# The first layer of the first expert, with the loop over input chunks outside three column groups

## The chip, the cores and the metric

The kernel runs on one core of a Trainium2 chip. The metric is the device time of one execution in microseconds (us). Three timed runs of the kernel before took 868.44, 870.32 and 873.09 us; their median is 870.32. Times inside the kernel come from one profiled execution.

## The reference

Capped attention followed by a mixture of experts, one expert for each token, all in float32:

```python
scores = scale * q @ k.T                   # 8 batches, 12 heads, 448 positions, head size 64
scores = cap * tanh(scores / cap)
attn = softmax(scores) @ v
x = attn as (3584, 768)                    # tokens x model width
logits = x @ w_gate + modality_bias[modality_id]
e = argmax(logits); gate = softmax(logits)[e]
out = gate * (relu(x @ w1[e]) @ w2[e])     # 8 experts, 768 -> 1024 -> 768
```

## The kernel before, in words

**Stages.** Attention comes first, in 24 units (`ND`) of two head pairs each, seven steps (`STEPS`) a unit, 168 steps in all. A step (`scores`, L443) has TensorE form scores, ScalarE take tanh and exp of them; `weigh` (L471) multiplies the weights with the values a few steps later, into a two-bank tile xT; `add` (L463, VectorE) sums the weights, `keep` (L486) copies xT out of PSUM, `sums` (L490) forms row sums and logits for the gate, `turn` (L501) transposes these, `logits` (L511) divides, `tokens` (L524) transposes the unit's output to token rows and writes them to the DRAM array xd. After three units a batch is complete, and `route` (L212) finds each token's expert and its place in a map in DRAM (mapd), with four indirect puts of 112 tokens each on GpSimd's queue.

Then come slots of up to 384 tokens of one expert. A slot's rows are fetched by three indirect gathers of 128 rows (`gather`, L710) through a piece of the map (mt) into xg. They are transposed in six chunks (`KC`) of 128 columns and split into a high and a low part (`transpose`, L743: ScalarE copies the high part, VectorE subtracts it from the whole to get the low). Weights are loaded by SyncE into four buffers (raw; two more, spare, for the first expert) and split likewise (`split_w`, L727). The first layer (`ffn1`, L762) has eight column groups (`FC`) of 128; each sums over six chunks three products, high by high, high by low and low by high. The second layer (`ffn2`, L793) runs six groups of 24 products.

**The seam.** The first slot belongs to an expert that has enough tokens already before the last batch. `SOON` is the unit (20 of 0 to 23) after which it is chosen. In unit 22 the map is made complete for it, `early_slot` (L292) picks it, SyncE starts to load its six first-layer chunks (`load_w1`, L558), and at step 4 of that unit GpSimd gathers its rows. Chunks 0 to 2 of its weights are split on GpSimd, chunk 3 on VectorE in unit 23, chunks 4 and 5 on ScalarE and VectorE behind the last step. After the last step, the code (L630 to L644) transposes chunks 0 to 3 into two double banks, then runs the last two `weigh`, then transposes chunks 4 and 5, adds and keeps. The first layer of the first slot then takes up what is left of attention in between: `last_sums`, `last_logits` and `last_rank` after column groups 0, 1 and 2, and the table of all later slots (`slots`, L310) after group 4. The first four second-layer weight chunks are split ahead of the column groups in program order, ScalarE casting and GpSimd subtracting (`load_w2`, L738).

**Order.** `pin` keeps an instruction in program order among the pinned ones of its engine; what isn't pinned is placed by a scheduler when the program is built. Semaphores and waits follow from which tiles are read and written. Each engine then works through its own queue in order. The first layer's products are not pinned; attention's are.

Of the kernel before, what the change touches and what calls it, by code (L numbers as in the profile page):

```python
# [69 lines left out]
W2_EARLY = 4  # L70
CAP_FAST = 64.0
# [7 lines left out]
class Program:  # L79
# [132 lines left out]
    def route(self, b, lg, pool, ps, tok=None, bank=None):  # L212

        nc = self.nc
        L = pool.tile([CP, C, E], F32, name="L")
# [26 lines left out]
        nc.vector.tensor_tensor(self.acc, before[:, C - 1], oh[:, C - 1], op=ALU.add)  # L242
        yield
# [8 lines left out]
        nc.vector.tensor_tensor(  # L252
            rows, rk.rearrange("p (c e) -> p c e", c=C), self.region[:CP].unsqueeze(1).to_broadcast([CP, C, E]), op=ALU.add
        )
        nc.vector.tensor_tensor(rows, rows, oh, op=ALU.mult)
        posf = pool.tile([CP, C], F32, name="posf")
        nc.vector.tensor_reduce(posf, rows, axis=AX.X, op=ALU.add)
        pos = pool.tile([CP, C], I32, name="pos")
        nc.vector.tensor_copy(pos, posf)

        pay = pool.tile([CP, C, 2], F32, name="pay" if tok is not None else f"pay{b % 2}")
        if tok is None:
            nc.gpsimd.iota(pay.bitcast(I32)[:, :, 0], pattern=[[1, C]], base=b * S, channel_multiplier=C)
        else:
            nc.vector.tensor_copy(pay.bitcast(I32)[:, :, 0], tok)
        gs = pool.tile([CP, C], F32, name="gs")
        nc.vector.tensor_reduce(gs, ex, axis=AX.X, op=ALU.add)
        nc.vector.tensor_scalar(gs, gs, 1e-9, None, op0=ALU.add)
        nc.vector.reciprocal(pay[:, :, 1], gs)
# [14 lines left out]
    def counts(self, pool, ps):  # L284
# [4 lines left out]
        nc.vector.tensor_copy(cnt, cps[:, :E])  # L289
# [128 lines left out]
    def attention(self, firsts, rp, xp):  # L418
        tc, nc = self.tc, self.nc
        pe, pin, V = nc.tensor, self.pin, nc.vector  # L420
        with ExitStack() as st:
            ld = st.enter_context(tc.tile_pool(name="ld", bufs=3))
            pp = st.enter_context(tc.tile_pool(name="pp", bufs=5))
            ps_s = st.enter_context(tc.tile_pool(name="ps_s", bufs=2, space=PSUM))
            ps_x = st.enter_context(tc.tile_pool(name="ps_x", bufs=1, space=PSUM))
            ps_g = st.enter_context(tc.tile_pool(name="ps_g", bufs=1, space=PSUM))

# [58 lines left out]
            def keep(d):  # L486
                kept[d] = xp.tile([128, 2, S], F32, name="xT", bufs=3)
                pin(V.tensor_copy(kept[d], self.xT[:, :, :S]))
# [60 lines left out]
            def start_route(b):  # L549
                way = self.route(b, lgs[b], rp, self.ps_r, bank=lambda: self.glog)  # L550
                next(way)
                routing[:] = [way]
# [21 lines left out]
            for n in range(END):  # L574
# [14 lines left out]
                if s == 4 and d >= 2:  # L589
                    if d - 2 == SOON:  # L590
                        self.gather(maps, known=NT - S)
                    else:
                        turn(d - 2)
# [36 lines left out]
            for n in due[END][:2]:  # L630
                weigh(n)
# [450 lines left out]
```

## Time and profile before

| | |
|---|---|
| profiled execution, its own time | 869.54 us |
| span, first to last instruction | 867.9 us |
| timed runs | median 870.32 us (868.44 to 873.09) |
| TensorE (PE) busy | 835.6 us, 96% |
| ScalarE (ACT) busy | 529.3 us, 61% |
| VectorE (DVE) busy | 515.4 us, 59% |
| GpSimd (POOL) busy | 153.2 us, 18% |
| mean granted TensorE clock | 0.990 |
| moved by DMA | 136.92 MB, 158 GB/s over the span |

A busy time says how long an engine had an instruction in work; matmuls overlap, two records at a time, so the start distance and not the duration is what one costs. The granted clock is 1.00 at 2.4 GHz and 0.50 at 1.2 GHz. A timeline row has start, duration, engine, line, operation, output <- inputs, shapes, how many instructions were merged into it and, in brackets, how long the engine had been idle before and what released it. PEld is TensorE's weight load, SP is SyncE, and a q behind an engine's name is its queue of issued instructions.

### The profile page before, as it was taken

Reading aid. Unit: us, or ns where it says so; the run is one execution under the profiler, and the core shown is the slowest. Engines: PE = TensorE matmul, PEld = TensorE weight load, DVE = VectorE, ACT = ScalarE, POOL = GpSimd, SP = SyncE. Lnnn points to the kernel's source line nnn. Section 1 sums busy time; section 2 is a strip of 40 time slices with the busy share of each in tenths; the row PEclk is TensorE's granted clock in tenths of the full one; section 3 lists DMA queues with packets and bytes.
Section 4 is the critical chain, followed back from the end, with each engine's and each line's share of the span. In section 5 each row is a group of like instructions: output and inputs, shape, how many; then the busy total and the mean of one; then the engine's idle time right before and its main releaser. Section 6 shows DMA issues by size and latency. Waiting matters only on the chain. (4 is left out here: it accounts for less than half of the span.)

```text
span 867.9 us, 15885 instructions
## 1 busy us (share of the span) xinstructions
PE 835.6 (96%) x6216; PEld 635.6 (73%) x6216; DVE 515.4 (59%) x889; ACT 529.3 (61%) x624; POOL 153.2 (18%) x161
## 2 busy tenths in 40 slices
PE   7999999999999995999999999999999999999996
PEld 2344444434444433989999999999999999989996
DVE  3679687888888788855443444234444433457851
ACT  6999999999999982244442444334344333446551
POOL 2002020202021154552020020201102030110000
PEclk9999999999999997999999999999999999999998
DMA  5353544554453664377255473534646354447650
GB/s 169 104 171 92 165 124 157 145 170 100 161 125 132 171 146 170 105 234 263 101 159 210 140 250 111 169 132 162 239 140 212 100 167 165 159 144 238 220 184 6
DMA packets 44284, 136.92 MB, mean 158 GB/s; under 512 B 8526, under 2 KB 9102, under 8 KB 44192
## 3 DMA queue, kind: packets, MB, share of 16 engines
q1 hardware_dynamic: 35008, 103.10, 37.4%
q0 software_dynamic: 9040, 32.64, 12.0%
q8 instruction: 52, 0.85, 0.4%
q14 instruction: 40, 0.33, 0.1%
q10 hardware_dynamic: 144, 0.00, 0.0%
HBM read 114.20 MB, written 22.69 MB: 158 GB/s over the span
## 5 line engine op out<-in xcount | busy, mean ns | idle before, releaser
L455 ACT ACTIVATE pt<-sc,isc 128x896 f32<-128x896 f32 x168 | 161.2, 994 | 14.4 <-PE sc L451 8.6
L781 PE MATMUL ph<-x,al 128*128 128x384 f32 (+2 forms) x528 | 166.8, 316 | 0.0
L806 PE MATMUL py<-bh,hh 128*128 128x384 f32 x464 | 158.7, 343 | 1.4 <-ACT hh L787 1.4
L806 PE MATMUL py<-bh,hl 128*128 128x384 f32 x464 | 156.3, 337 | 0.0
L806 PE MATMUL py<-bl,hh 128*128 128x384 f32 x464 | 156.0, 337 | 0.0
L458 ACT ACTIVATE pt<-pt,cabs 128x1792 f32<-128x1792 f32 x84 | 150.4, 1790 | 2.7
L481 PE MATMUL xT<-pt,va 64*64 64x448 f32 x1344 | 147.2, 542 | 0.0
L469 DVE TENSOR_TENSOR tot<-tot,pt 128x896 f32<-128x896 f32 x120 | 134.8, 1123 | 7.2 <-ACT pt L458 3.9
L777 PE MATMUL ph<-x,ah 128*128 128x384 f32 x384 | 128.9, 336 | 0.0
L778 PE MATMUL ph<-x,ah 128*128 128x384 f32 x384 | 128.6, 335 | 0.0
L481 PEld LDWEIGHTS xT<-pt,va 64*64 64x64 f32 x1344 | 50.6, 134 | 78.2 <-issue 69.0
L732 DVE TENSOR_TENSOR bl<-raw,bh 128x768 fp32r<-128x768 f32 x84 | 77.6, 956 | 48.6 <-ACT bh L731 48.4
L731 ACT CAST bh<-raw 128x768 fp32r<-128x768 f32 x88 | 70.0, 839 | 58.3 <-DMA raw<-in_w_dram 49.5
L781 PEld LDWEIGHTS ph<-x,al 128*128 128x128 f32 x528 | 100.7, 191 | 0.0
L816 POOL DMA_INDIRECT out_dram<-ot,mt x29 | 32.5, 1120 | 383.9 <-ACT ot L811 308.4
L811 ACT ACTIVATE ot<-py,mt 128x384 f32<-128x384 f32 x58 | 33.7, 581 | 98.7 <-PE py L806 53.1
L787 ACT ACTIVATE hh<-ph 128x384 fp32r<-128x384 f32 x64 | 30.5, 488 | 99.4 <-PE ph L781 95.7
L806 PEld LDWEIGHTS py<-bh,hh 128*128 128x128 f32 x464 | 87.2, 188 | 1.8 <-ACT hh L787 1.7
L732 DVE TENSOR_TENSOR al<-raw,ah 128x1024 fp32r<-128x1024 f32 x61 | 74.7, 1256 | 22.1 <-ACT ah L731 22.0
L806 PEld LDWEIGHTS py<-bl,hh 128*128 128x128 f32 x464 | 87.2, 188 | 0.3 <-DVE bl L732 0.2
L760 DVE TENSOR_TENSOR x<-ptr,x 128x384 fp32r<-128x384 f32 (+2 forms) x66 | 32.8, 517 | 92.0 <-ACT x L759 92.0
L806 PEld LDWEIGHTS py<-bh,hl 128*128 128x128 f32 x464 | 87.2, 188 | 0.2 <-DVE hl L788 0.2
(156 smaller groups left out, 1056.0 us busy)
## 6 DMA issues: line engine op xcount, KB each, us to landing
raw<-in_w_dram SPq DMA_DIRECT2D x88, 384.0 KB, 4.9
raw<-in_w_dram SPq DMA_DIRECT2D x64, 512.0 KB, 4.5
kq<-in_kq_dram SPq DMA_DIRECT2D x24, 448.0 KB, 5.6
va<-in_v_dram SPq DMA_DIRECT2D x24, 448.0 KB, 6.7
kx<-in_kq_dram SPq DMA_DIRECT2D x24, 448.0 KB, 5.8
xd<-xs POOLq DMA_DIRECT2D x23, 448.0 KB, 4.8
spare<-in_w_dram SPq DMA_DIRECT2D x2, 512.0 KB, 7.3
mapd<-pay,pos POOLq DMA_INDIRECT x32, 8.3
```

Source lines behind the costliest of these rows:

```text
L455: pin(nc.scalar.activation(weights(n), sc[:, :, :S], AF.Tanh, scale=self.isc))
L458: pin(nc.scalar.activation(pt, pt, AF.Exp, scale=self.cabs))
L469: pin(V.tensor_tensor(tots[d], pt_of(n - 1) if s == 1 else tots[d], pt_of(n), op=ALU.add))
L481: pin(pe.matmul(self.xT[j * D : (j + 1) * D, i, :S], vas[d][rows, o : o + D], pt[rows, j], start=s == 0, stop=s == STEPS - 1,))
L731: keep((cast.tensor_copy if cast else self.nc.scalar.copy)(hi, raw))
L732: keep((minus or self.nc.vector).tensor_tensor(lo, raw, hi, op=ALU.subtract))
L760: keep(nc.vector.tensor_tensor(lo, pt[:, :w], hi, op=ALU.subtract))
L777: nc.tensor.matmul(ph[:, :w], hi[:, fs], self.x[:, k, 0, :w], start=first, stop=False)
L778: nc.tensor.matmul(ph[:, :w], hi[:, fs], self.x[:, k, 1, :w], start=False, stop=False)
L781: nc.tensor.matmul(ph[:, :w], lo[:, fs], self.x[:, k, 0, :w], start=False, stop=last)
L806: nc.tensor.matmul(py[:, :HALF], self.h[a][:, f, rows], self.w2s[f][c][:, cs], start=i == 0, stop=i == 3 * FC - 1,)
L811: nc.scalar.mul(ot[:, cs], py[:, :HALF], mt[:, t, 1:2])
```

## The change

In the first slot alone, the first layer's loop over chunks now stands outside its first three column groups: for each chunk, nine products into three banks, then what has to happen before the next chunk. The other five groups run as before, one after the other. The products of the first four groups are pinned.

- `transpose` is divided into `move` (TensorE) and `take` (ScalarE and VectorE). Before the layer only chunk 0 is moved and taken, and chunks 1 and 2 moved, each into a bank of its own; chunks 3 to 5 are moved at the layer's start (`move_last`) and taken between the chunks' products (`ready`). The pool of score banks is closed earlier for that.
- Weight chunks 0 and 1 are split on VectorE alone in units 22 and 23, chunks 2 to 5 on ScalarE and VectorE, chunk 2 behind the last step and 3 to 5 between the chunks' products. GpSimd splits none of the first layer's.
- The last `keep` moves from VectorE to ScalarE, and the last four additions are divided around chunk 0.
- The gather of the first slot is issued at step 2 of unit 22, not step 4. The sums of unit 21 move from step 5 of unit 22 to step 0 of unit 23.
- What is left of attention hangs on other places: sums after chunk 2, logits after chunk 3, the last batch's routing after the three groups, its rank after group 3; the slot table stays after group 4. The second-layer weight chunks are split two after the three groups and two after group 3. Of the second layer's weight loads three are issued before the layer and one after chunk 3's split.
- In `route`, the gate weights are computed before the rank, and for the batch of the first slot the whole tail is pinned (`firm`).

```diff
@@ route
-    def route(self, b, lg, pool, ps, tok=None, bank=None):
+    def route(self, b, lg, pool, ps, tok=None, bank=None, firm=False):
+        firmly = self.pin if firm else (lambda inst: inst)
...
+        firmly(nc.vector.tensor_reduce(gs, ex, axis=AX.X, op=ALU.add))
+        firmly(nc.vector.tensor_scalar(gs, gs, 1e-9, None, op0=ALU.add))
+        firmly(nc.vector.reciprocal(pay[:, :, 1], gs))
         yield
...
+        firmly(nc.vector.tensor_reduce(posf, rows, axis=AX.X, op=ALU.add))
+        firmly(nc.vector.tensor_copy(pos, posf))
@@ attention, steps
-                if s == 4 and d >= 2:
-                    if d - 2 == SOON:
-                        self.gather(maps, known=NT - S)
-                    else:
...
+                if (d, s) == (SOON + 3, 0):
+                    sums(d - 2)
...
                     load_w1((2, 3, 4, 5))
-                    split(0, nc.gpsimd, nc.gpsimd)
-                if (d, s) == (SOON + 2, 4):
-                    split(1, nc.gpsimd, nc.gpsimd)
-                    split(2, nc.gpsimd, nc.gpsimd)
-                if (d, s) == (SOON + 3, 4):
-                    split(3, V, V)
+                    self.gather(maps, known=NT - S)
+                if (d, s) == (SOON + 2, 6):
+                    split(0, V, V)
+                if (d, s) == (SOON + 3, 5):
+                    split(1, V, V)
@@ attention, behind the last step
+            sst.close()
+            ps_m = st.enter_context(tc.tile_pool(name="ps_m", bufs=4, space=PSUM))
+            free = [ps_m.tile([128, 512], F32, name="ptr") for _ in range(4)]
+            spots = (
+                ps_g.tile([128, 512], F32, name="ptr", tag="glog"), free[3],
+                self.ps_r.tile([128, 512], F32, name="ptr", tag="small"),
+            )
+            left = due[END]
+            for n in left[:2]:
                 weigh(n)
+            for n in range(END - BEHIND, END - 2):
+                add(n)
+            self.move(0, spots[0])
+            self.take(0, spots[0], pin=True)
+            for k in (1, 2):
+                self.move(k, spots[k])
+            for n in left[2:]:
                 weigh(n)
+            keep(ND - 1, nc.scalar.copy)
+            add(END - 2)
+            add(END - 1)
+            self.take(1, spots[1], pin=True)
+            split(2, None, V)
+            self.take(2, spots[2], pin=True)
+            self.raws = [self.load_raw(self.first_e, self.w2, k, DM) for k in range(3)]
+            def move_last():
+                for k, pool in zip(range(3, KC), (self.ps_t, self.ps_t, self.ps_y)):
+                    last.append(pool.tile([128, 512], F32, name="ptr" if k < 5 else "py"))
+                    self.move(k, last[-1])
+            def ready(k):
+                if k >= 3:
+                    split(k, None, V)
+                    self.take(k, last[k - 3], pin=True)
+                if k == 3:
+                    self.raws.append(self.load_raw(self.first_e, self.w2, k, DM))
             def last_sums():
+                ready(3)
                 sums(ND - 1, self.ps_y, "py")
                 turn(ND - 2)
                 logits(ND - 2)
-                tokens(ND - 2, nc.gpsimd, *[(self.ps_t, "ptr")] * 2)
             def last_logits():
+                ready(4)
                 turn(ND - 1)
                 logits(ND - 1)
+            def last_route():
+                tokens(ND - 2, nc.gpsimd, *[(self.ps_t, "ptr")] * 2)
                 self.way = self.route(B - 1, lgs[B - 1], rp, self.ps_r)
...
+                "start": move_last, ("k", 2): last_sums, ("k", 3): last_logits, ("k", 4): lambda: ready(5),
+                ("k", KC - 1): last_route, ("f", 3): last_rank,
@@ ffn1
+        if lead:
+            hooks["start"]()
+            phs = [bank() for _ in range(lead)]
+            for k in range(KC):
+                for f in range(lead):
+                    products(phs[f], f, k)
+                if k < KC - 1:
+                    hook("k", k)
+            for f in range(lead):
+                finish(phs[f], f)
+            hook("k", KC - 1)
+        for f in range(lead, FC):
+            ph = bank()
+            for k in range(KC):
+                products(ph, f, k)
+            finish(ph, f)
+            hook("f", f)
@@ run_slot
+            early = lambda ks: self.load_w2(cur[0], raws, ks, self.nc.gpsimd)
+            for at, ks in ((("k", KC - 1), range(2)), (("f", 3), range(2, W2_EARLY))):
+                hooks[at] = lambda work=hooks[at], ks=ks: (work(), early(ks))
```

## Rows read from the trace of the kernel before

**Rows 1.** Busy time by stretches of 20 us: stretch, length, busy us (and instructions) of PE, PEld, DVE, ACT and POOL, then the mean granted TensorE clock, the share of the DMA engines and GB/s.

```profile
320.00:340.00 20.00, 10.59 (x92) 5.24 (x96) 15.31 (x15) 9.44 (x11) 12.59 (x8) 0.80 0.75 266
```

**Rows 2.** TensorE's timeline over the seam: L506 turn, L495 sums, L481 attention products, L750 transposes of token rows, L777 the first layer's first product.

```profile
319.91 0.65 PE L506 MATMUL lt<-ident,gl 128*112 128x128 f32 x4
...
322.28 0.57 PE L495 MATMUL glog<-tot,pick 128*32 128x448 f32 x2
...
323.97 3.94 PE L481 MATMUL xT<-pt,va 64*64 64x448 f32 x40
330.17 0.25 PE L750 MATMUL ptr<-identr,xg 128*128 128x128 f32 x1 [2.26 <-DMA xg<-xd,mt]
...
333.15 0.37 PE L750 MATMUL ptr<-identr,xg 128*128 128x128 f32 x1 [1.37 <-DMA xg<-xd,mt]
336.96 1.00 PE L750 MATMUL ptr<-identr,xg 128*128 128x128 f32 x6 [3.44 <-DVE x L760]
339.21 0.62 PE L750 MATMUL ptr<-identr,xg 128*128 128x128 f32 x3 [1.25 <-DVE x L760]
339.76 2.90 PE L481 MATMUL xT<-pt,va 64*64 64x448 f32 x16
...
343.13 0.41 PE L777 MATMUL ph<-x,ah 128*128 128x384 f32 x1
```

**Rows 3.** The list of waits between 326 and 344 us: who waited for whom, us in total, times, the longest.

```profile
PEld ptr L750 <- DVE x L760: 5.1, 2, 3.6
PE ptr L750 <- DMA xg<-xd,mt: 4.7, 3, 2.3
```

**Rows 4.** VectorE's timeline: L259 the places of the tokens in the map, L469 additions of attention, L731 a weight cast, L760 the low part of a transposed chunk.

```profile
303.55 0.17 DVE L259 CAST pos<-posf 112x4 int32<-112x4 f32 x1
...
308.95 1.08 DVE L469 TENSOR_TENSOR tot<-pt 128x896 f32<-128x896 f32 x1
...
310.66 7.26 DVE L469 TENSOR_TENSOR tot<-tot,pt 128x896 f32<-128x896 f32 x4
...
325.00 1.96 DVE L731 CAST ah<-raw 128x1024 fp32r<-128x1024 f32 x1 [1.97 <-DMA raw<-in_w_dram]
...
332.57 2.73 DVE L469 TENSOR_TENSOR tot<-tot,pt 128x896 f32<-128x896 f32 x1
...
336.37 0.54 DVE L760 TENSOR_TENSOR x<-ptr,x 128x384 fp32r<-128x384 f32 x1
```

**Rows 5.** ScalarE's timeline: L759 the high part of chunk 0.

```profile
333.56 0.48 ACT L759 CAST x<-ptr 128x384 fp32r<-128x384 f32 x1 [5.52 <-PE ptr L750]
```

**Rows 6.** GpSimd's timeline: L272 the puts into the map (first and fourth of one batch, fourth of the last batch), L732 a weight subtraction, L713 gathers (first and third of the first slot, first of the second), L704 the map read for the second slot.

```profile
304.53 0.99 POOL L272 DMA_INDIRECT mapd<-pay,pos  x1 [8.07 <-DVE esc L304]
...
308.36 2.49 POOL L272 DMA_INDIRECT mapd<-pay,pos  x1 [0.30 <-issue]
...
313.85 3.13 POOL L732 TENSOR_TENSOR al<-raw,ah 128x1024 fp32r<-128x1024 f32 x1
321.63 1.08 POOL L713 DMA_INDIRECT xg<-xd,mt  x1 [4.66 <-DMA mt<-mapd]
...
324.34 1.01 POOL L713 DMA_INDIRECT xg<-xd,mt  x1 [0.30 <-issue]
...
365.88 0.94 POOL L272 DMA_INDIRECT mapd<-pay,pos  x1 [0.30 <-issue]
...
371.35 0.54 POOL L704 DMA_DIRECT2D mt<-mapd  x1 [0.81 <-issue]
...
375.04 1.43 POOL L713 DMA_INDIRECT xg<-xd,mt  x1 [0.40 <-issue]
```

**Rows 7.** Busy time in short stretches, columns as in rows 1; the last three are granted clock, DMA share and GB/s.

```profile
332.00:333.00 1.00, 0.00 (x0) 0.00 (x0) 1.00 (x3) 0.00 (x0) 1.00 (x1) 0.50 0.07 28
...
340.00:342.00 2.00, 2.00 (x12) 0.56 (x12) 1.23 (x2) 1.30 (x2) 0.00 (x0) 0.50 0.00 0
342.00:344.00 2.00, 2.00 (x19) 1.41 (x12) 0.96 (x2) 0.86 (x2) 0.00 (x0) 0.96 0.00 0
```

**Rows 8.** Groups of instructions over the whole run, shapes kept apart: line, engine, operation, tiles and shapes, count, then busy us, mean ns of one, and the idle time before them.

```profile
L455 ACT ACTIVATE pt<-sc,isc 128x896 f32<-128x896 f32 x168 | 161.2, 994 | 14.4 <-PE sc L451 8.6 <-DVE meta L371 5.7
...
L732 DVE TENSOR_TENSOR al<-raw,ah 128x1024 fp32r<-128x1024 f32 x61 | 74.7, 1256 | 22.1 <-ACT ah L731 22.0
...
L731 ACT CAST ah<-raw 128x1024 fp32r<-128x1024 f32 x60 | 60.6, 1049 | 25.5 <-DMA raw<-in_w_dram 22.3 <-PE py L806 1.3 <-DVE al L732 1.3
...
L760 DVE TENSOR_TENSOR x<-ptr,x 128x384 fp32r<-128x384 f32 x54 | 29.1, 554 | 83.8 <-ACT x L759 83.8
...
L499 DVE COPY gl<-glog 128x448 f32<-128x448 f32 x24 | 14.9, 620 | 0.1
...
L732 POOL TENSOR_TENSOR bl<-raw,bh 128x768 fp32r<-128x768 f32 x4 | 7.2, 1835 | 15.0 <-ACT bh L731 15.0
```

**Rows 9.** The same table as rows 1 for the first layer of the first slot.

```profile
343.10:372.25 29.15, 29.15 (x182) 27.88 (x181) 22.71 (x92) 7.33 (x14) 13.64 (x12) 1.00 0.29 86
```

**Rows 10.** TensorE's timeline at the second slot's first transposes.

```profile
385.84 0.28 PE L750 MATMUL ptr<-identr,xg 128*128 128x128 f32 x1 [0.65 <-DMA xg<-xd,mt]
387.53 0.53 PE L750 MATMUL ptr<-identr,xg 128*128 128x128 f32 x4 [1.41 <-DMA xg<-xd,mt]
```

More of the change, by code (lines that the diff above doesn't have):

```diff
@@ L633, in attention @@
-            pair = [ps_s.tile([128, 2, 512], F32, name="ptr", tag="sc") for _ in range(2)]
-            for k in range(4):
-                move(k, pair[k // 2][:, k % 2])
-            for n in due[END][2:]:
-                weigh(n)
-            split(5, None, V)
-            move(4, self.ps_r.tile([128, 512], F32, name="ptr", tag="small"))
-            move(5, ps_g.tile([128, 512], F32, name="ptr", tag="glog"))
-            for n in range(END - BEHIND, END):
-                add(n)
-            keep(ND - 1)
@@ L741, in load_w2, with move @@
             self.split_w(raw, self.w2s[k], pin=bool(raws), minus=minus)
[L743 to L748 removed]
+    def move(self, k, pt, n=TW):
         for t in range(n):
[L750 removed]
+            move = self.nc.tensor.transpose(
                 pt.bitcast(F32R)[:, t * 128 : (t + 1) * 128], self.xg[:, t, k * 128 : (k + 1) * 128], self.identr
@@ L754, in transpose, with take, ffn1 @@
                 self.pin(move)
+    def take(self, k, pt, n=TW, pin=False):
+        nc, w = self.nc, n * 128
+        keep = self.pin if pin else (lambda inst: inst)
         hi, lo = self.x[:, k, 0, :w], self.x[:, k, 1, :w]
-        if busy:
-            keep(nc.vector.tensor_copy(hi, pt[:, :w]))
-        else:
-            keep(nc.scalar.copy(hi, pt[:, :w]))
+        keep(nc.scalar.copy(hi, pt[:, :w]))
         keep(nc.vector.tensor_tensor(lo, pt[:, :w], hi, op=ALU.subtract))
-    def ffn1(self, n, between=()):
+    def transpose(self, k, pool, tag, n=TW):
+        pt = pool.tile([128, 512], F32, name="ptr", tag=tag)
+        self.move(k, pt, n)
+        self.take(k, pt, n)
+    def ffn1(self, n, hooks=None):
         nc = self.nc
@@ L769, in ffn1, with products, finish @@
         hh, hl = self.h
[L770 to L781 removed]
+        bank = lambda: self.ps_h.tile([128, 512], F32, name="ph")
+        lead = LEAD if hooks else 0
+        def products(ph, f, k):
+            hi, lo = self.w1s[k]
+            keep = self.pin if hooks and f <= lead else (lambda inst: inst)
+            fs = slice(f * 128, (f + 1) * 128)
+            first, last = k == 0, k == KC - 1
+            if n == TW:
+                keep(nc.tensor.matmul(ph[:, :w], hi[:, fs], self.x[:, k, 0, :w], start=first, stop=False))
+                keep(nc.tensor.matmul(ph[:, :w], hi[:, fs], self.x[:, k, 1, :w], start=False, stop=False))
+            else:
+                nc.tensor.matmul(ph[:, : 2 * w], hi[:, fs], self.x[:, k, :, :w], start=first, stop=False)
+            keep(nc.tensor.matmul(ph[:, :w], lo[:, fs], self.x[:, k, 0, :w], start=False, stop=last))
+        def finish(ph, f):
             acc = ph[:, :w]
@@ L788, in ffn1, with hook @@
             nc.vector.scalar_tensor_tensor(hl[:, f, :w], acc, 0.0, hh[:, f, :w], op0=ALU.max, op1=ALU.subtract)
-            for at, work in between:
-                if at == f:
-                    work()
+        def hook(*at):
+            if hooks and at in hooks:
+                hooks[at]()
+        if lead:
[15 more added lines that the diff above has]
+            hook("f", f)
     def ffn2(self, mt, n, between=(), wait=0):
```

96 lines of the change are left out of this document (37 added, 59 removed).

## The prediction, made before the result was known

> **What bounds the kernel now.** Read first the busy table by stretches [rows 1]: between 320 and 340 us TensorE is busy 10.59 of 20 us, at a mean granted clock of 0.80, while the stages on either side keep it full. That is the seam between attention and the first expert, and the only stretch with a large hole. Next, TensorE's own timeline over that seam [rows 2]. Attention's last products end at 323.97 + 3.94 = 327.91; the first matmul of the expert's first layer stands at 343.13. Between them lie 18 transposes and two steps of attention products, about 3.5 us of work at full clock, in 15.2 us.
>
> The list of waits says who is late [rows 3]. First the gather of the token rows: 4.7 us in three waits; its third part lets chunk 0's last transpose go at 333.15. I call this moment G. Then VectorE's subtraction of a transposed chunk (L760), 5.1 us on the weight-load side. The timelines say why: ScalarE has chunk 0's high part at 333.56 + 0.48 = 334.04 [rows 5], but VectorE takes the low part only at 336.37 [rows 4], as it is behind with additions of attention, one of which takes 2.73 us where 1.08 is usual [rows 4]. Chunks 0 and 1 share a two-bank tile, so TensorE waits for that subtraction before it transposes chunk 1 (336.96) [rows 2]. From G + 0.37 = 333.52 to 343.10 the seam takes 9.58 us. From 343.10 to 372.25 TensorE is busy throughout, 29.15 us [rows 9]: 182 records, 144 of them products and the other 38, some 4 us, logits, turns and token transposes.
>
> **The change, part by part.**
>
> *Until G.* The three weight splits leave GpSimd; two go to VectorE during attention, 2 x (cast + subtraction). The cast without a neighbour on GpSimd is not shown: 1.05 to 1.96 us, by ScalarE's cast of that shape and VectorE's beside a busy GpSimd [rows 4, 8]; I take 1.2, nearer the undisturbed one, and 1.256 for the subtraction [rows 8]. About 5 us are added, the split of chunk 3 that leaves this place takes 3.2 or more away (1.96 and a subtraction), and what GpSimd's subtractions cost the additions (7.26 us for four, 2.9 over 4 x 1.08) comes back [rows 4]. The first waits for its weights, and what queues behind it on VectorE is additions and the copies that free the product banks. Any delay they bring ScalarE's loop is covered until G: TensorE had 2.2 us of idle time before the first transpose at 330.17 [rows 2]. If the cover goes, the excess counts one for one.
>
> G itself hangs on the map: four puts from 304.53, the map read, three gathers from 321.63 to 324.34 [rows 6]. The pinned order of the routing helps the first put: the positions were done at 303.55 + 0.17, and it started 0.81 later [rows 4, 6]; at best 0.8 us is won. The move of the gather two steps up passes only the first split's two instructions on GpSimd's queue, and it then waits for the map anyway: nothing. Against it: VectorE was idle for 1.97 us up to 325.00 [rows 4], beside gathers two and three, and now has an addition, a copy and a split there. A gather beside VectorE took 1.43 against 1.01 [rows 6], so 0.4 us each for two; the bound is the fourth put, 2.49 against 0.94. I take the two effects as equal: G stays at 333.15, with -0.8 and +1.6 for the range. On SyncE the loads keep their order; the second-layer loads two and three come later, as their buffers are freed by splits that now run inside the first layer, and they are not needed before its fourth column group.
>
> *From G to the first product.* Chunk 0's last transpose 0.37; six transposes of chunks 1 and 2, each now with a bank of its own, 1.00 at half clock [rows 2], the 1.2 GHz level (granted 0.50 [rows 7]). Then 16 records of attention products: 2.90 at half clock, 40 take 3.94 at full, so 16 take 1.6 [rows 2]. The clock had fallen by 332 us and was back at about 342, some 3 us after TensorE had resumed at 339.21 [rows 2, 7]. With work unbroken from G it would be back in the middle of these products: 2.3. The nine transposes of chunks 3 to 5 then lie beside ScalarE's copy of the product bank, which the first column groups need: 0.99, as the tanh of the same shape (L455) [rows 8], plus 0.05 to start. Sum 0.37 + 1.00 + 2.3 + 1.04 = 4.7: first product at 337.9 against 343.1, **-5.2 us** (-5.9 with the products at full clock, -4.5 at half).
>
> *Inside the three column groups.* The work is the same; a chunk is 9 products of 0.174 = 1.56 us (29.15 less 4 over 144 [rows 9]). Between chunks stand, as before in other places, the sums (eight records; four lie over each other in some 0.5 us, so 1.0) and two turns (0.65 each) [rows 2]. New is that VectorE must feed each chunk. From 337.9, ScalarE needs 0.48 for each chunk's high part and 1.05 for each weight cast, VectorE 0.55 and 1.256 for the low parts [rows 5, 8], in a fixed order. Walked through: low parts of chunk 1 at 338.95, chunk 2 at 341.2 (needed 341.2), chunk 3 at 343.0 (needed 344.5). VectorE then owes logits work of a copy of 0.62 [rows 8] and a reciprocal and two small products, some 0.7 together, so chunk 4 comes at 346.9 (needed 346.75) and, after the second logits, chunk 5 at 349.4 (needed 348.5). Waits 0.2 + 0.15 + 0.9, **+1.2 us**. Bounds: 0, and 2.5 if each of some twelve handovers costs 0.1 more. The fourth column group needs the first bank; the eight token transposes placed there cover its relu and subtraction. The remaining five groups run as now. The layer ends 4.0 us earlier, at 368.2.
>
> *After the layer.* The second slot's gather is late today: TensorE waits 0.65 + 1.41 us for it [rows 10]. Its chain is map puts to 365.88, map read 371.35, gathers from 375.04, that is 6.4 before, 0.9 before and 2.8 after the layer's end [rows 6]. The puts keep their distance to the layer's end, but GpSimd's four subtractions for the second layer, now two and two, stand among them. One of 1.835 us [rows 8] ahead of the puts, or two after them in front of the slot table's write, moves the gather by about 0.4; I take **+0.4**, between 0 and 2.3.
>
> Sum: -5.2 + 1.2 + 0.4 = -3.6 us. The profiled execution took 869.54 (span 867.9 and 1.6 around it): 865.9. The three timed runs have a median of 870.32, 0.8 above it, and the forecast is made on that: **866.7 us**.
>
> **The rivals.**
>
> *GpSimd's gathers are held up by VectorE, and it gets slower.* The place: 321.6 to 326 us. The price: the put that started just ahead of an addition took 2.49 where one without took 0.94, so 1.5 more [rows 4, 6]. For three gathers 4.6 us, on G, and then all attention products run at half clock, 0.5: -3.6 + 5.1 = +1.5, **871.8**. It decides from 3.6 us on. Against it: the first gather meets only the scaling of transposed tokens, with one operand in PSUM, and the 1.43 us rows. The Trainium skill ("SBUF — State Buffer", section "Who interferes with whom") has a VectorE instruction with two SBUF inputs contend with a GpSimd one that reads SBUF, the second to issue blocked until the first ends; by that rule the additions and the split would each cost their length. Rows 4 and 6 agree for the 2.49 us put, while the 1.43 us gathers fall short of a full block.
>
> *The gain is given back at the second slot.* GpSimd takes all its subtractions ahead of the puts: the puts end 2.3 us later against the layer's end, and beside VectorE each subtraction grows, as 1024 columns took 3.13 us [rows 6], 2.3 for 768: one more. The wait of 2.06 becomes 5.4: -4.0 + 3.3 = -0.7, **869.6**. For it: GpSimd's queue is in order, and the casts for it come early. Against it: the puts stand first in the program.
>
> *More is gained.* The clock does not stay low after G, the puts gain their 0.8 and no chunk waits: -5.9 - 0.8 = -6.7, **863.6**. Against it: TensorE has the same sparse 4 us before G.
>
> **How the numbers follow.** Chances: forecast 0.52 (its own -2.2 to -5.0), more gained 0.18, given back 0.18, slower 0.12. The range of 862.5 to 870.9 reaches to both sides of the rivals and leaves out most of the slower case and the tail of the best. About 0.5%, 4.35 us, is what a measurement of this kernel can tell from no change. Below 865.97 lie all of the large gain and a third of the forecast: 0.18 + 0.18 = 0.36. Above 874.67 lies only the slower case with more delays on it: 0.06. The rest, 0.58, is within 0.5%.
>
> **What would show it.** Right: G within 1.6 us of 333.15; the six transposes in one piece behind it; first product near 338; a hole near 1 us before the sixth chunk's products; the layer over near 368; a wait of 2 to 3 us at the second slot's transposes; everything later shifted by the sum. Wrong: gathers of 1.5 us and more with G at 335 or later; waits at every chunk, VectorE full between them; the layer over by 368 but the second slot waiting 4 us or more; attention ending after 330.

## The result and the profile after

The changed kernel is slower. Nineteen timed runs of it against twenty of the kernel before gave a ratio of 1.0061, with a 95% interval of 1.0045 to 1.0077, that is 5.3 us (3.9 to 6.7) on 870; the medians are 876.29 and 870.1 us. A twentieth run of it took 1686.29 us, about twice the others, and is left out. Forecast were 866.7 us and a range up to 870.9.

The profiled execution after took 872.72 us (span 871.1), 3.2 more than the one before. It is a favourable one: in the profile before, the granted clock falls once more late in the run (0.83 in 840:850 us), in this one it does not. The marks below are therefore taken inside the trace, up to the second slot's transposes, the last work that the change touches.

TensorE's timeline after, the answer to [rows 2] and [rows 10]. Lines are those of the changed kernel: L484 attention products, L773 transposes of token rows, L805 the first layer's products, L498 sums, L257 and L259 the rank, L537 token transposes, L855 the second layer.

```profile
323.97 3.94 PE L484 MATMUL xT<-pt,va 64*64 64x448 f32 x40
...
332.05 1.13 PE L773 MATMUL ptr<-identr,xg 128*128 128x128 f32 x7 [1.46 <-DMA xg<-xd,mt]
333.11 3.27 PE L484 MATMUL xT<-pt,va 64*64 64x448 f32 x16
338.38 1.00 PE L773 MATMUL ptr<-identr,xg 128*128 128x128 f32 x6 [2.00 <-DVE x L784]
339.56 0.65 PE L805 MATMUL ph<-x,ah 128*128 128x384 f32 x1
...
354.25 1.04 PE L537 MATMUL tp<-ident,xT 128*112 128x128 f32 x8
...
359.68 0.22 PE L257 MATMUL rank<-oh,tri 112*112 112x32 bf16 x1 [1.25 <-DVE oh L237]
360.30 0.18 PE L259 MATMUL rank<-before,ones 112*112 112x32 bf16 x1 [0.40 <-DVE before L243]
...
373.88 0.34 PE L855 MATMUL py<-bh,hh 128*128 128x384 f32 x1
...
378.39 0.45 PE L855 MATMUL py<-bl,hh 128*128 128x384 f32 x1 [1.92 <-DVE bl L760]
...
391.78 0.54 PE L773 MATMUL ptr<-identr,xg 128*128 128x128 f32 x4 [1.32 <-DMA xg<-xd,mt]
```

Read the brackets first. G (332.05) is 1.1 us earlier than before, and the first product (339.56) 3.6 us earlier. The second layer, though, starts at 373.88, 1.6 us later than before, and the second slot's third part at 391.78, 4.25 later. So the gain is there at the front, and more than all of it is lost behind. New waits stand at four places: 2.00 ahead of chunk 3's transposes, 1.25 and 0.40 for the rank, 1.92 in the second layer.

The same engine by stretches; the last three columns are granted clock, DMA share and GB/s [rows 7].

```profile
334.00:336.00 2.00, 2.00 (x16) 0.41 (x8) 1.62 (x2) 0.00 (x0) 0.00 (x0) 0.50 0.00 0
342.00:344.00 2.00, 2.00 (x8) 2.00 (x7) 0.00 (x1) 1.04 (x2) 0.00 (x0) 0.50 0.75 221
378.00:382.00 4.00, 3.61 (x12) 3.61 (x13) 2.94 (x4) 0.00 (x0) 1.94 (x4) 0.59 0.61 155
```

TensorE is full in 342:344, and yet only 8 products fall into these 2 us, in part or whole: they start 0.32 us apart, so that six start where eleven would at 0.174. The level of 0.50 lasts until about 344.5, through the attention products and 15 products of the layer. After the 1.92 us wait it falls a second time.

VectorE's and GpSimd's timelines in the last part of the layer: L231, L252 and L237 the last batch's routing, L341 the slot table, L818 the layer's low part, L760 weight subtractions.

```profile
356.67 1.10 DVE L231 SCALAR_TENSOR_TENSOR sc<-L,desc 112x32 f32<-112x32 f32 x1
...
357.91 1.62 DVE L252 TENSOR_SCALAR gs<-gs 112x4 f32<-112x4 f32 x1
359.44 0.18 DVE L237 TENSOR_TENSOR oh<-sc,first 112x32 bf16<-112x32 f32 x1
...
366.85 4.94 DVE L341 TENSOR_TENSOR nbig<-nbig,early 128x8 f32<-128x8 f32 x1
...
376.47 1.00 DVE L818 SCALAR_TENSOR_TENSOR hl<-ph,hh 128x384 fp32r<-128x384 f32 x2
377.40 3.54 DVE L760 TENSOR_TENSOR bl<-raw,bh 128x768 fp32r<-128x768 f32 x4
```

```profile
355.87 3.63 POOL L760 TENSOR_TENSOR bl<-raw,bh 128x768 fp32r<-128x768 f32 x2 [29.82 <-ACT bh L759]
...
367.98 3.78 POOL L760 TENSOR_TENSOR bl<-raw,bh 128x768 fp32r<-128x768 f32 x2
376.51 0.61 POOL L382 DMA_DIRECT2D metad<-metai  x1 [4.76 <-DVE plan L408]
```

Add starts and durations. VectorE's instruction on 112x4 numbers ends at 357.91 + 1.62 = 359.53, GpSimd's pair at 359.50; the one on 128x8 numbers ends at 371.79, GpSimd's second pair at 371.76. Instructions of 0.2 us last until GpSimd is done, and what queues behind them (the rank, the rest of the slot table, the low parts of the second layer's chunks 4 to 7) is late with them. The Trainium skill ("SBUF — State Buffer", section "SBUF: two separate sides") calls the port pair of these two engines an exclusive lock, held for a whole instruction; by that rule an instruction of VectorE that needs these ports waits for the end of the GpSimd instruction that has them. The trace agrees for L231 and L252: GpSimd's four subtractions take 1.82 to 1.98 us each, so the first ends at about 357.7 and the second at 359.50, and the two VectorE instructions end at 357.77 and 359.53. The 4.94 us end with the lock too, but they are longer than both subtractions together (3.78).

### The profile page after: what moved, and what is told of

The parts are those of the page before. It is cut to its first block, busy times and chain, and to the rows that moved or that the text cites. A ratio compares the mean times of both kernels' runs of the same rounds, so it can differ in the third digit from the quotient of the medians.

```text
span 871.1 us, 15881 instructions
## 1 busy us (share of the span) xinstructions
PE 838.6 (96%) x6216; PEld 637.6 (73%) x6216; DVE 516.9 (59%) x892; ACT 531.8 (61%) x627; POOL 140.0 (16%) x155
## 5 line engine op out<-in xcount | busy, mean ns | idle before, releaser
L855 PE MATMUL py<-bh,hh 128*128 128x384 f32 x464 | 159.0, 343 | 0.9 <-ACT hh L817 0.9
L855 PE MATMUL py<-bl,hh 128*128 128x384 f32 x464 | 156.5, 338 | 1.9 <-DVE bl L760 1.9
L855 PE MATMUL py<-bh,hl 128*128 128x384 f32 x464 | 156.7, 338 | 0.0
L484 PE MATMUL xT<-pt,va 64*64 64x448 f32 x1344 | 147.5, 543 | 0.0
L472 DVE TENSOR_TENSOR tot<-tot,pt 128x896 f32<-128x896 f32 x120 | 130.3, 1086 | 7.2 <-ACT pt L461 3.9
L805 PE MATMUL ph<-x,ah 128*128 128x384 f32 x384 | 129.9, 338 | 0.0
L484 PEld LDWEIGHTS xT<-pt,va 64*64 64x64 f32 x1344 | 50.5, 134 | 78.2 <-issue 68.8
L760 DVE TENSOR_TENSOR bl<-raw,bh 128x768 fp32r<-128x768 f32 x84 | 77.5, 955 | 49.8 <-ACT bh L759 47.1
L759 ACT CAST bh<-raw 128x768 fp32r<-128x768 f32 x88 | 70.1, 840 | 54.6 <-DMA raw<-in_w_dram 48.5
L760 DVE TENSOR_TENSOR al<-raw,ah 128x1024 fp32r<-128x1024 f32 x64 | 76.3, 1223 | 22.6 <-ACT ah L759 22.3
L855 PEld LDWEIGHTS py<-bl,hh 128*128 128x128 f32 x464 | 87.7, 189 | 2.2 <-DVE bl L760 2.2
L855 PEld LDWEIGHTS py<-bh,hh 128*128 128x128 f32 x464 | 87.5, 189 | 1.3 <-ACT hh L817 1.2
L855 PEld LDWEIGHTS py<-bh,hl 128*128 128x128 f32 x464 | 87.6, 189 | 0.1
```

The costliest lines, as they stand in the source:

```text
L472: pin(V.tensor_tensor(tots[d], pt_of(n - 1) if s == 1 else tots[d], pt_of(n), op=ALU.add))
L484: pin(pe.matmul(self.xT[j * D : (j + 1) * D, i, :S], vas[d][rows, o : o + D], pt[rows, j], start=s == 0, stop=s == STEPS - 1,))
L759: keep((cast.tensor_copy if cast else self.nc.scalar.copy)(hi, raw))
L760: keep((minus or self.nc.vector).tensor_tensor(lo, raw, hi, op=ALU.subtract))
L805: keep(nc.tensor.matmul(ph[:, :w], hi[:, fs], self.x[:, k, 0, :w], start=first, stop=False))
L855: nc.tensor.matmul(py[:, :HALF], self.h[a][:, f, rows], self.w2s[f][c][:, cs], start=i == 0, stop=i == 3 * FC - 1,)
```

## The experiments

Three theories of the loss, and a fourth from the first four runs:
- **A**: GpSimd's subtractions, now two and two among the routing and the slot table, hold VectorE up.
- **B**: the clock, low through the first 15 products because TensorE is nearly idle from 327.9 us to G.
- **C**: chunk 3's transposes wait for chunk 1's low part, as chunk 1 lies in a bank that chunk 3 takes next.
- **D**: once the layer is earlier, chunk 4 of the second layer waits for the last token rows to land in xd.

Runs differ by up to 4 us before the seam, so the marks are counted from the start of attention's last 40 products (323.97 in the timeline above): first product, second layer's first product, third part of the second slot's transposes. Ratios are to the kernel before on the same chip. Marks come from one profiled execution each, ratios from six runs or more, and the two need not agree: the trace of e1_fill is of the shortest of twelve runs (867.43 us, the longest 876.1), that of e7_all of the longest of six (866.21 us, the shortest 862.01).

| run | first product | second layer | second slot | ratio (95%) |
|---|---|---|---|---|
| before | 19.16 | 48.28 | 63.56 | 1 |
| after | 15.59 | 49.91 | 67.81 | 1.0061 (1.0045 to 1.0077) |
| e1_fill | 13.13 | 45.14 | 62.72 | 1.0018 (0.9999 to 1.0037) |
| e2_bank | 15.58 | 50.00 | 67.39 | 1.0041 (1.0023 to 1.0060) |
| e3_w2_vector | 15.27 | 47.67 | 63.42 | 0.9996 (0.9981 to 1.0012) |
| e4_three | 13.12 | 44.82 | 61.49 | 0.9988 (0.9973 to 1.0003) |
| e5_before_fill | 19.31 | 49.04 | 64.14 | 0.9989 (0.9974 to 1.0005) |
| e6_bank | 13.63 | 46.17 | 63.16 | 1.0010 (0.9992 to 1.0028) |
| e7_all | 12.55 | 43.21 | 58.10 | 0.9928 (0.9906 to 0.9950) |
| e8_nofill | 13.59 | 44.55 | 59.52 | 0.9948 (0.9928 to 0.9969) |
| e9_no_d | 11.67 | 42.31 | no wait there | 0.9956 (0.9938 to 0.9973) |
| e10_gpsimd | 11.66 | 43.47 | 58.34 | 0.9955 (0.9937 to 0.9972) |
| e11_before_fixed | 19.18 | 48.93 | 63.68 | 0.9999 (0.9980 to 1.0017) |
| e12_rows_only | 11.73 | 42.38 | 56.95 | 0.9940 (0.9917 to 0.9963) |

**e1_fill**, the clock alone:

```diff
+            for _ in range(24):
+                pin(pe.matmul(free[3][:, :W], self.ones[:, :128], self.ones, start=True, stop=True))
             self.move(0, spots[0])
```

> The kernel after, with 24 small matmuls of ones put on TensorE between the end of attention's products and the first transpose, into a bank that chunk 1 takes later. They compute nothing that is used. Theory B (the granted clock, low from about 332 to 344.5 us because TensorE does next to nothing from 327.9 until G, costs much of the time): the clock stays near 1.00 through the seam, the transposes and attention products behind G take 0.4 + 1.6 us and not 1.13 + 3.27, and the first 15 products of the layer stand 0.174 and not 0.32 us apart; first product some 2 us earlier, end some 4 us earlier, about 1.0015 of the kernel before, where after had 1.0061. Theories A (GpSimd's second-layer subtractions slow VectorE) and C (chunk 3 shares a bank with chunk 1): little or nothing changes, 1.005 to 1.007; C expects the wait of 2.0 us ahead of the transposes of chunk 3 to stay, whatever the clock.

1.0018, as B says. TensorE's timeline (the ones at L641, transposes L775, attention products L484) and its clock behind G:

```profile
328.15 4.07 PE L641 MATMUL ptr<-ones 112*128 112x384 bf16 x24
331.92 1.01 PE L775 MATMUL ptr<-identr,xg 128*128 128x128 f32 x9
332.86 1.73 PE L484 MATMUL xT<-pt,va 64*64 64x448 f32 x16
336.60 0.70 PE L775 MATMUL ptr<-identr,xg 128*128 128x128 f32 x6 [2.00 <-DVE x L786]
```

```profile
338.00:342.00 4.00, 4.00 (x25) 4.00 (x24) 2.22 (x4) 3.26 (x6) 0.00 (x0) 1.00 0.62 150
```

The attention products take 1.73 and not 3.27 us, the clock stays at 1.00, the first product comes 2.5 us sooner and the second layer 4.8. The wait of 2.00 is unchanged, as C said. The mean granted clock of this execution is 0.997, that of the other eleven 0.988 to 0.995, so the trace shows what the matmuls can bring and not what they brought each time.

**e2_bank**, another bank for chunk 1 in the same pool:

```diff
-                ps_g.tile([128, 512], F32, name="ptr", tag="glog"), free[3],
+                ps_g.tile([128, 512], F32, name="ptr", tag="glog"), free[1],
...
+            pin(pe.matmul(free[0][:, :W], self.ones[:, :128], self.ones, start=True, stop=True))
             self.move(0, spots[0])
```

> The kernel after, with chunk 1 transposed into a bank that chunk 3 does not use (one small matmul of ones is added to the same end; it computes nothing that is used). Theory C: the wait of 2.00 us ahead of chunk 3's transposes goes, the first product stands at about 337.5 and not 339.56, and the end moves by 2 us: 1.0035 to 1.004 of the kernel before. Theory B: the clock still falls from 332 us on, and the first 15 products still stand 0.32 us apart, so that no more than the 2 us come. Theory A: the waits behind the three column groups (1.25 and 0.40 us for the rank, 1.92 us at the second layer) stay.

A miss for C as stated: chunk 1 now lies in another bank of the pool, and the wait is the same to the hundredth.

```profile
338.46 1.00 PE L774 MATMUL ptr<-identr,xg 128*128 128x128 f32 x6 [2.00 <-DVE x L785]
```

The first product did not move (15.58). The ratio fell a little, but its interval overlaps that of the kernel after.

**e3_w2_vector**, A alone:

```diff
-            early = lambda ks: self.load_w2(cur[0], raws, ks, self.nc.gpsimd)
+            early = lambda ks: self.load_w2(cur[0], raws, ks)
```

> The kernel after, with the low parts of the second layer's first four weight chunks subtracted on VectorE and not on GpSimd. Theory A: VectorE's routing and slot-table instructions lose their stretch (the 4.94 us instruction of the slot table falls under 1 us), the rank's waits of 1.25 and 0.40 us and the second layer's wait of 1.92 us go, and with them the second fall of the clock, some 2 us: 5 to 5.5 us earlier, 1.000 of the kernel before. Theory B alone: the rank's waits may shrink, the first half of the seam does not change: 1.004 to 1.006. Rival to A: VectorE has no room for four more subtractions of about 1 us, the waits move to the low parts or to the rank, and nothing comes: 1.005 or more.

0.9996, as A says; the rival (no room on VectorE) falls. VectorE's timeline, the rows of above and its new subtractions:

```profile
356.17 0.17 DVE L252 TENSOR_SCALAR gs<-gs 112x4 f32<-112x4 f32 x1
...
356.54 0.96 DVE L760 TENSOR_TENSOR bl<-raw,bh 128x768 fp32r<-128x768 f32 x1
...
364.81 0.16 DVE L341 TENSOR_TENSOR nbig<-nbig,early 128x8 f32<-128x8 f32 x1
```

1.62 is 0.17 and 4.94 is 0.16. The rank's waits are gone, the second layer's 1.92 has become 0.22 + 0.37, and the second slot stands 4.4 us earlier than in the kernel after.

**e4_three**: the edits of e2_bank and e3_w2_vector, and 24 matmuls of ones into free[0].

> The three edits together: 24 small matmuls of ones that compute nothing used, chunk 1 in a bank of its own, the second layer's first low parts on VectorE. If A, B and C each hold and add up: 4 + 2 + 5 us off the kernel after, 865 us, 0.994 of the kernel before. If only A holds: 1.000. If C holds only together with B (the wait is hidden behind slow attention products otherwise): below 0.996.

0.9988, less than the sum of the three: 0.7 us better than e3_w2_vector alone, within both intervals. The first product is 2.2 us earlier than there (relative marks), the second layer 2.9, and then the gain stops. ScalarE, TensorE and GpSimd at that place:

```profile
371.92 3.04 ACT L761 CAST bh<-raw 128x768 fp32r<-128x768 f32 x4 [2.52 <-DMA metad<-metai]
```

```profile
372.80 0.62 PE L857 MATMUL py<-bh,hh 128*128 128x384 f32 x2 [1.85 <-ACT bh L761]
```

```profile
365.35 0.76 POOL L546 DMA_DIRECT2D xd<-xs  x1
```

Twelve products into the second layer TensorE waits for chunk 4's high part, and ScalarE had idled 2.52 us before casting it. The list names the slot table's write (metad). But chunk 4's buffers lie where attention's token rows lay, and the last of those are sent at 365.35, behind four map puts. The list of transfers (KB, then us from issue to landing) has them landed 6.3 us later, at 371.65; the cast starts at 371.92:

```profile
xd<-xs POOLq DMA_DIRECT2D x1, 448.0 KB, 6.3
```

In the kernel before, the same two instructions are 6.0 us apart, with ScalarE's last relu (372.45, 0.49 us) ending just at the cast: there it cost nothing.

```profile
366.82 0.76 POOL L543 DMA_DIRECT2D xd<-xs  x1
```

```profile
372.84 3.04 ACT L731 CAST bh<-raw 128x768 fp32r<-128x768 f32 x4
```

That is theory D. This kernel also still had the 2.00 us wait, and the clock fell behind it (0.50 in 338:340) in spite of the matmuls of ones. In e1_fill's trace it did not, with the same matmuls and the same wait; why is open.

**e5_before_fill**, a control in the kernel before:

```diff
+            for _ in range(24):
+                pin(pe.matmul(pair[0][:, 0, :W], self.ones[:, :128], self.ones, start=True, stop=True))
             for k in range(4):
```

> The kernel before, with the same 24 small matmuls of ones (they compute nothing used) between attention's last products and the first transpose of the seam. Theory B (the clock): the clock is near 1.00 at G, the seven transposes and 16 attention products behind it go from 1.0 + 2.9 to about 0.7 + 1.7 us unless the clock falls again in the 3.4 us wait for VectorE; first product 1 to 2 us earlier than 343.13. Theory D (new: chunk 4 of the second layer can be cast only when the last token rows have landed in xd, since its buffer lies where they were; in the run with three edits ScalarE waited 2.5 us for that): of this gain at most some 0.8 us is kept, since the last rows land at 366.82 + 5.2 = 372.0 and the cast stands at 372.84. So 0.998 to 0.9995; without D 0.9975.

0.9989, no difference that can be told from 1. The first product did not come earlier (19.31), so this says nothing on D: TensorE's idle time moved into the wait for VectorE, and the clock fell there.

```profile
335.62 1.00 PE L752 MATMUL ptr<-identr,xg 128*128 128x128 f32 x6 [4.27 <-DVE x L762]
```

**e6_bank**, chunk 1 in a pool of its own, and chunk 5 transposed behind the first chunk's products:

```diff
-            ps_m = st.enter_context(tc.tile_pool(name="ps_m", bufs=4, space=PSUM))
-            free = [ps_m.tile([128, 512], F32, name="ptr") for _ in range(4)]
+            ps_i = st.enter_context(tc.tile_pool(name="ps_i", bufs=3, space=PSUM))
+            idle = [ps_i.tile([128, 512], F32, name="idle") for _ in range(3)]
+            ps_m = st.enter_context(tc.tile_pool(name="ps_m", bufs=1, space=PSUM))
...
+            for n in range(3):
+                pin(pe.matmul(idle[n % 3][:, :W], self.ones[:, :128], self.ones, start=True, stop=True))
...
-                "start": move_last, ("k", 2): last_sums, ...
+                "start": move_last, ("k", 0): lambda: move_last((5,)), ("k", 2): last_sums, ...
```

> The kernel after, with chunk 1 in a bank whose pool of tiles no early tile of the layer follows: chunks 3 and 4 are moved at the layer's start as before, chunk 5 behind the first chunk's products; three small matmuls of ones that compute nothing used take the place of the unused banks. In e2_bank the bank alone was changed and the wait of 2.0 us stayed, so the wait is for the whole pool. Theory C in its new form: the wait of 2.0 us goes, the first product stands at about 337.5, as soon as ScalarE has copied attention's product bank (336.44 + 0.91), and the end comes some 2 us earlier: 1.0035 to 1.0045 of the kernel before. Rival: the clock stays low for as long from a start 2 us earlier, or the rest is held by VectorE and GpSimd behind the three groups (A), and less than 1 us comes: 1.005 or more.

The wait is gone. Chunk 5's transposes stood behind it, so their later place is not the reason. With e2_bank, this says that a tile of the next pool waits for every user of the pool that it follows, not for its own bank alone. The first product comes 2.0 us earlier in relative marks, and the second layer 3.7, more than the 2 expected:

```profile
331.89 1.13 PE L776 MATMUL ptr<-identr,xg 128*128 128x128 f32 x7 [1.27 <-DMA xg<-xd,mt]
...
337.24 0.45 PE L808 MATMUL ph<-x,ah 128*128 128x384 f32 x1
```

```profile
336.00:338.00 2.00, 1.91 (x14) 1.58 (x11) 0.40 (x1) 1.72 (x3) 0.00 (x0) 0.74 0.00 0
338.00:342.00 4.00, 4.00 (x27) 3.96 (x26) 3.45 (x5) 4.00 (x7) 0.00 (x0) 1.00 0.31 76
```

With no break behind 331.89 the clock is back before 338, in the kernel after only at 344.5. So the wait cost its 2 us and most of the slow products as well: B and C are not independent.

**e7_all**: the pool of e6_bank with 24 matmuls of ones, the VectorE line of e3_w2_vector, and against D

```diff
             def last_rank():
-                next(self.way, None)
                 tokens(ND - 1, nc.gpsimd, *[(self.ps_t, "ptr")] * 2)
+                next(self.way, None)
...
-                        self.run_slots(early, {**hooks, ("f", 4): order})
+                        rank = hooks["f", 3]
+                        self.run_slots(early, {**hooks, ("f", 3): lambda: (rank(), order())})
```

> The kernel after with five edits: chunk 1's pool as in e6_bank, 24 small matmuls of ones that compute nothing used, the second layer's first low parts on VectorE, and, against theory D, the last token rows written ahead of the four map puts on GpSimd's queue and the slot table started one column group earlier. If D is right: the wait of 1.85 us that the run with three edits had in the second layer goes, the second slot's gather comes about 3 us earlier, and the time is 864 to 866 us, 0.994 to 0.996 of the kernel before. If D is wrong: the wait stays, 0.998 to 0.999.

0.9928, better than both kernels: 6.3 us under the kernel before and about 11.5 under the kernel after. The second slot's mark is 5.5 us earlier than before. The rows go out at 356.11, and no wait stands in the second layer:

```profile
356.11 0.67 POOL L546 DMA_DIRECT2D xd<-xs  x1 [3.66 <-DVE rows L263]
```

**e8_nofill**: e7_all with 3 matmuls of ones, not 24.

> e7_all with 3 small matmuls instead of 24. Theory B: the clock falls before G and comes back in the layer's first products, 3 to 4 us of the gain go, 0.998 to 1.000 of the kernel before. If the clock is worth nothing: as e7_all.

0.9948, between its two forecasts, and its interval overlaps that of e7_all: the marks say 1.0 us at the first product and 1.4 at the second slot, less than the 3 to 4 expected of B, as the work behind G is now unbroken and the clock is back soon. Part of it is hidden by G, which stands 0.8 us later against the mark in e7_all's trace (9.06 and 8.24). G and what follows it in e7_all and in e8_nofill:

```profile
332.54 0.80 PE L776 MATMUL ptr<-identr,xg 128*128 128x128 f32 x7 [0.99 <-DMA xg<-xd,mt]
```

```profile
332.57 1.13 PE L776 MATMUL ptr<-identr,xg 128*128 128x128 f32 x7 [1.48 <-DMA xg<-xd,mt]
```

The first product stands at 336.03 and at 337.92, so from G the matmuls of ones bring 1.9 us.

**e9_no_d, e12_rows_only**: e7_all without the last two edits, and with only the one that sends the rows ahead of the puts.

> e7_all without its two edits against theory D: the last token rows go out behind the four map puts again and the slot table starts a column group later; chunk 1's pool, the 24 small matmuls and the low parts on VectorE stay. Theory D: the second layer begins at about the time of e7_all (366.7), but its 13th product cannot stand before the last rows have landed (about 371) and chunk 4 is cast and subtracted, so TensorE waits 2 to 4 us there, or at the second slot's transposes, and the time is 0.997 to 0.999 of the kernel before, as with the three edits of e4_three although the first product is earlier. If D is wrong (chunk 1's pool made the difference between e4_three and e7_all): 0.993 to 0.994.

> e9_no_d with only the last token rows put ahead of the map puts (the slot table stays where the kernel after has it). Theory D as stated (the landing of the rows holds the cast): the wait in the second layer goes, the second slot's gather stays late by the table: 0.995 to 0.997. If the table's write holds the cast, as the list of waits names it: no better than e9_no_d.

e9_no_d waits in the second layer as e4_three did, 1.56 us, and its clock falls to 0.57 behind that:

```profile
372.85 0.62 PE L858 MATMUL py<-bh,hh 128*128 128x384 f32 x2 [1.56 <-ACT bh L762]
```

```profile
374.00:378.00 4.00, 4.00 (x15) 4.00 (x16) 2.40 (x3) 1.00 (x2) 3.38 (x4) 0.57 0.79 273
```

Its table and cast:

```profile
368.28 0.61 POOL L382 DMA_DIRECT2D metad<-metai  x1 [1.84 <-DVE plan L408]
```

```profile
371.97 3.03 ACT L762 CAST bh<-raw 128x768 fp32r<-128x768 f32 x4 [2.24 <-DMA metad<-metai]
```

e12_rows_only has neither the wait nor the fall, and its cast starts without a wait:

```profile
368.18 0.62 POOL L382 DMA_DIRECT2D metad<-metai  x1 [2.51 <-DVE plan L408]
```

```profile
369.97 3.04 ACT L762 CAST bh<-raw 128x768 fp32r<-128x768 f32 x4
```

That is 1.8 us behind the start of the table's write, where e9_no_d's stood 3.7 behind it (368.28 and 371.97). So the write of the table does not hold the cast, although the list of waits names it; the rows do, as nothing else differs. In time the two (0.9956 and 0.9940) are not apart: e9_no_d lies between its two forecasts and e12_rows_only below its own, so D rests on the traces. The table's earlier start shows no gain over e12_rows_only.

**e10_gpsimd**: e7_all with GpSimd's subtractions back.

> e7_all with the second layer's first low parts subtracted on GpSimd again, as in the kernel after. Theory A: the two subtractions behind the three column groups stretch VectorE's routing again (one instruction of 1 us and one of 1.6 us where 0.2 is usual) and the rank's waits of 1.25 and 0.40 us come back; the other two now stand behind the slot table on GpSimd's queue, ahead of the second slot's map reads, and make its gather about 3.7 us later. 2 to 5 us lost against e7_all: 0.995 to 0.999. If A is wrong: 0.993.

0.9955, 2.4 us above e7_all, as A says, with a small overlap of the intervals. Counted from the first product, the second layer comes 1.15 us later than in e7_all (31.81 and 30.66), the second slot 1.1 (46.68 and 45.55). The rank's waits are back, if smaller, and so is VectorE's long instruction, which ends at 356.15, GpSimd's pair at 356.13. L341 takes 0.15 us here, as GpSimd's second pair now stands behind the slot table:

```profile
356.30 0.18 PE L257 MATMUL rank<-oh,tri 112*112 112x32 bf16 x1 [0.39 <-DVE oh L237]
356.93 0.18 PE L259 MATMUL rank<-before,ones 112*112 112x32 bf16 x1 [0.45 <-DVE before L243]
```

```profile
354.51 1.64 DVE L252 TENSOR_SCALAR gs<-gs 112x4 f32<-112x4 f32 x1
```

**e11_before_fixed**: the kernel before with the ones of e5_before_fill, the rows ahead of the puts and the table after group 3.

> The kernel before with what can be taken over from e7_all without the change: the 24 small matmuls that compute nothing used, the last token rows ahead of the map puts, the slot table one column group earlier. If what made e7_all fast is these edits and not the change, it comes near e7_all: 0.994 to 0.995. If the change is worth its 4 us once its new waits are gone, this one keeps the first product at 342 to 343 and gains only at the second slot's gather, where the kernel before waits 0.65 + 1.41 us: 0.997 to 0.999.

0.9999: without the change no gain of these edits can be told. The wait for VectorE in the seam (4.23 us) stays, and the first product with it (19.18). The subtractions on VectorE are not among them; what those would do in the kernel before was not tested.

## Why the prediction was wrong, step by step

*Until G.* Right in kind: G came 1.1 us earlier, just past the -0.8 that was given as the best. It was not won at the puts, which start at 304.53 in both traces; the first gather starts at 320.69 against 321.63 [rows 6]. Why was not tested. The gathers took 1.05, 1.02 and 1.91 us; only the third was longer than before (1.01), and G came earlier, so the rival that had them held up falls.

*From G to the first product.* Forecast 4.7 us, measured 339.56 - 332.05 = 7.5. Two terms failed. The attention products took 3.27 and not 2.3: the clock did not come back in their middle. The nine transposes were to lie beside ScalarE's copy (1.04, measured 0.06 + 0.91): they stand behind it, after 1.03 more of waiting, and cost 1.18 of their own. The six transposes of chunks 1 and 2 did go in one piece. The step that failed is "The nine transposes of chunks 3 to 5 then lie beside ScalarE's copy": it took their banks for free, and e2_bank and e6_bank show that it is the pool that counts.

*Inside the three column groups.* The feared waits (1.2) were 0.32. What was left out is the clock: 15 products 0.32 us apart instead of 0.174 are 2.2 us. The groups took 14.7 against a forecast of 12.85.

*"The remaining five groups run as now."* This sentence was the worst: with the four subtractions alone taken off GpSimd (e3_w2_vector), the ratio goes from 1.0061 to 0.9996, 5.7 us. The five groups took 2.2 us more than forecast, 1.65 of it the rank's two waits. Their instructions are the old ones, but their neighbours on GpSimd are new. The prediction weighed VectorE and GpSimd against each other at the gathers, and let the subtractions grow beside VectorE, but it never let VectorE's routing and slot table wait for the subtractions that the change sets beside them. e3_w2_vector and e10_gpsimd show this.

*After the layer.* The rival that had the gain given back by GpSimd's subtractions named the right instructions and the wrong victim: it priced the map puts behind them on GpSimd's queue, which kept their distance. VectorE's slot table paid, then the second layer's chunks 4 to 7 (1.92 us) and the clock after that wait. From the second layer's start to the second slot's third part it took 17.9 us against a forecast of 15.7. The last wait there (1.32 us) is for the gather, which follows the table. The table's write and the third gather in the kernel before, and the third gather after (its table stands at 376.51):

```profile
369.93 0.61 POOL L380 DMA_DIRECT2D metad<-metai  x1 [2.35 <-DVE plan L406]
378.49 1.01 POOL L713 DMA_INDIRECT xg<-xd,mt  x1 [0.30 <-issue]
```

```profile
384.31 1.00 POOL L741 DMA_INDIRECT xg<-xd,mt  x1 [0.30 <-issue]
```

The table is 6.6 us later and the gather 5.8. So the late table sets this mark; without the 1.92 us and the slow products TensorE would have come to it sooner and waited longer.

In sum 1.7 + 1.8 + 2.2 + 2.2 = 7.9 us over the -3.6 forecast, or +4.3; the timed runs say +5.3 (3.9 to 6.7).

*What would have failed anyway.* Even with the layer over at 368.2, as forecast, the full gain would not have been kept: e4_three reached its second layer 3.5 us earlier than before and lost 1.85 there again. The forecast followed the second slot's gather and not the reuse of the buffers under chunk 4, whose cover in the kernel before was ScalarE's own queue.

The idea itself held: with the obstacles A to D out of the way the same loop order is worth 5 to 6 us (e7_all, e12_rows_only), which e11_before_fixed does not get without it.

## What to carry to other kernels

Work that is moved takes its neighbours with it: for every stretch that "runs as now", list what the other engines do in it after the change, above all GpSimd's arithmetic beside a chain of small VectorE instructions. A bank or buffer is free when everything that its allocation waits for is free, so read which earlier tiles a new pool follows before counting on overlap. And when a stage ends sooner, follow each buffer that is handed over there; the next limit can be a transfer that had been covered without showing as a wait.

## What was not expected of the hardware

The instruction of 4.94 us is recorded from 366.85, 1.1 us before GpSimd's pair begins (367.98), while a put and a transfer were being issued there; e1_fill shows the same (4.94 from 362.38). Its end fits the lock; its start is not explained. An instruction with a single input (L252, 112x4) was held just as those with two. And with each of two short waits, 2.00 and 1.92 us, went a loss of about the same size through the granted clock: 15 and some 10 products stood 0.32 instead of 0.174 us apart, 2.2 and 1.5 us.
